# Moving the first weight columns to SyncE's queue, and reordering the start of an attention and feed-forward kernel

## The chip, the cores and the metric

One core of a Trainium2 chip. The metric is the device time of one execution in microseconds (us), lower is better. A profile gives the span of one execution; the timed value is about 2 us above the span. TensorE multiplies, VectorE and ScalarE copy and scale, GpSimd issues most DMAs, SyncE a few. In profile lines these are PE, DVE, ACT, POOL and SP; PEld is TensorE's weight load.

## The reference

Chunked attention (chunks of 32 tokens, 16 to the left and 8 to the right, 8 memory tokens), then a feed-forward part with a gate.

```python
for c in range(nc):                                   # batch 4, heads 8, 768 tokens, head size 64
    k_full = concatenate([mem_k, k[:, :, l_start:r_end]], axis=2)
    v_full = concatenate([mem_v, v[:, :, l_start:r_end]], axis=2)
    scores = matmul(q_c, k_full.T) / sqrt(64)
    out[:, :, c_start:c_end] = matmul(softmax(scores), v_full)
x = out.transpose(0, 2, 1, 3).reshape(3072, 512)
gate, val = maximum(x @ w_gate, 0), x @ w_val         # 512 x 1536 each
y = (gate * val) @ w_out                              # 1536 x 512
```

## The kernel before

Tokens go in 8 blocks of 384; heads go in pairs (`hp` 0 to 3). Everything in question is the first block, block 0, ahead of which nothing runs. Its rows of q, k and v (`rq`, `rk`, `rv`) come from GpSimd's queue, which casts f32 to f16 on the way; the first two heads come through SyncE and ScalarE as f32 (`kst`, `qst`), to start sooner. GpSimd's DMAs in order:

```python
load_k(0, 2, 2)                       # block 0, from head 2, 2 heads
load_rows_mem(pool_dma, ...)          # memory keys
load_q(0, 2, 2)
load_k(0, 4, 4)                       # the last four heads in one piece
load_q(0, 4, 4)
pool_dma(rv[0:KR], ...)               # the values of all 8 heads in one piece
load_rows_mem(pool_dma, rv[KR:KR + 2], 0, 0, H, mem_v)
load_w(0, 256)                        # the first 256 columns of wg and wv
load_w(256, 512)
# ... selection masks, the rows of block 1, further weights
```

`turn_pe` transposes rows of a head pair on TensorE, `step_s0` makes the scores and the exponentials, `wide_d` the sums (two ScalarE passes follow: log, then exponential), `gather_v` picks the value windows, `wide_v` multiplies by them, and VectorE scales the result into `xT`. The feed-forward part then takes `xT` in `chunk(0, f)`, four matmuls of the first two column blocks each; `fill` is a matmul whose result nobody reads.

```python
turn_pe(0, 1); turn_copy(0, 1)
step_s0(0, 0); step_s0(0, 1)
turn_pe(0, 2); turn_copy(0, 2)
wide_d(0, 0)
turn_pe(0, 3); turn_copy(0, 3)
step_s0(0, 2)
wide_d(0, 1)
step_s0(0, 3)
gather_v(0)                           # windows 0, 1 of all heads: 8 matmuls, one VectorE copy
wide_d(0, 2)
gather_v(2)                           # windows 2, 3
# ...
wide_v(0, 0)
wide_v(0, 1, xo2[:, 0, 0:TB])
# ... GpSimd's further loads
ffn_open(0, (0, 1))
wide_d(0, 3)
wide_v(0, 2)
chunk(0, 0); chunk(0, 1)
wide_v(0, 3, xo2[:, 1, 0:TB])
chunk(0, 2); chunk(0, 3)
```

The softmax here doesn't subtract the row's maximum and nothing guards it: scores larger than these inputs give would overflow.

Of the kernel before, what the change touches and what calls it, by code (L numbers as in the profile page):

```python
# [8 lines left out]
F32 = mybir.dt.float32  # L9
# [8 lines left out]
def kernel(  # L18
# [12 lines left out]
    nc = tc.nc  # L31

    B, H, S, D = q.shape
# [7 lines left out]
    TB = 384  # L41
    NB = B * S // TB
    NQ = 4
# [3 lines left out]
    J = 4  # L47
    QR = TB // J
    KR = 112
    NFC = DM // 128  # L50
# [3 lines left out]
    NEG = -30000.0  # L54

    const = ctx.enter_context(tc.tile_pool(name="const", bufs=1))
    half = ctx.enter_context(tc.tile_pool(name="half", bufs=2))
    turned = ctx.enter_context(tc.tile_pool(name="turned", bufs=2))
    epool = ctx.enter_context(tc.tile_pool(name="epool", bufs=4))
# [10 lines left out]
    sp = nc.sync.dma_start  # L70
    act_dma = nc.scalar.dma_start
    pool_dma = nc.gpsimd.dma_start
    dve_copy, act_copy = nc.vector.tensor_copy, nc.scalar.copy
# [2 lines left out]

    ident = const.tile([128, 128], F16, name="ident")
    sels = [const.tile([128, NQ, 32], F16, name=f"sel{p}") for p in range(2)]
    kst = const.tile([KR + 2, 2, J * D], F32, name="kst")
    qst = const.tile([QR, 2, J * D], F32, name="qst")  # L80
    k16s = [const.tile([128, NQ, H, D], F16, name=f"k16{p}") for p in range(2)]

    vwins = [const.tile([128, NQ, H, 2 * D], F16, name=f"vwin{p}") for p in range(2)]
# [3 lines left out]
    rv = const.tile([KR + 2, H, J * D], F16, name="rv")  # L87
# [39 lines left out]
    def load_k(n, h0, nh):  # L127
        pool_dma(rows_of(n)[0][0:KR, h0:h0 + nh], k_rows(n, h0, nh))  # L128

    def load_q(n, h0, nh):  # L130
        pool_dma(rows_of(n)[1][:, h0:h0 + nh], q_rows(n, h0, nh))

    def load_rows(n, h0, nh):
        load_k(n, h0, nh)
        load_q(n, h0, nh)
# [35 lines left out]
    def load_w(c0, c1):  # L171
        for dst, src in ((wg, moe_w_gate), (wv, moe_w_val)):
            pool_dma(dst[:, :, c0:c1], src.rearrange("(c p) f -> p c f", p=128)[:, :, c0:c1])
# [10 lines left out]
    def turn_pe(n, hp):  # L184
        if n != 1:
            pool, tag = (pools["t"], "t") if n == 0 else (pools["s"], "sc")
            ps = pool.tile([128, 2, 512], F32, tag=tag, name="kq_ps")
            kps, qps = ps[:, 0], xs if (n, hp) == (0, 0) else ps[:, 1, 0:TB]
        else:
            ps, kps, qps = None, bank("k_ps"), bank("q_ps")[:, 0:TB]  # L190
        turns[n, hp] = ps, kps, qps
        rk, rq = (t.rearrange("p h (j d) -> p h j d", j=J) for t in rows_of(n))
        sel = sels[n % 2].rearrange("p i t -> p (i t)")


        ksteps, qsteps = (dst.rearrange("p (j r) -> p j r", j=J) for dst in (kps, qps))
        if n == 0:
            ksteps = kps.rearrange("p (i j t) -> p j i t", i=NQ, j=J)
            qsteps = qps.rearrange("p (r j) -> p j r", j=J)
        for t, steps, w in ((rk, ksteps, sel[0:KR + 2]), (rq, qsteps, ident[:QR, :QR])):  # L200
            for j in range(J):
                for hh in range(2):
                    nc.tensor.matmul(steps[D * hh:D * hh + D, j], lhsT=t[:, 2 * hp + hh, j], rhs=w,  # L203
                                     start=True, stop=True)

    def turn_copy(n, hp):
        if n not in kTs:
            kq = turned.tile([128, HP, 512 + TB], F16, tag="kq", name="kq")
            kTs[n] = kq[:, :, 0:512].rearrange("p a (i m) -> p i a m", i=NQ)
            qTs[n] = kq[:, :, 512:].rearrange("p a (i m) -> p i a m", i=NQ)  # L210
            turns[n] = kq
        ps, kps, qps = turns.pop((n, hp))
        if n == 0 and hp == 0:
            dve_copy(turns[n][:, hp, 0:512], kps)
            act_copy(q00, qps)
        elif n == 0:
            dve_copy(turns[n][:, hp], ps.rearrange("p a c -> p (a c)")[:, 0:512 + TB])
        else:
            for src, dst in ((kps, turns[n][:, hp, 0:512]), (qps, turns[n][:, hp, 512:])):
                dve_copy(dst.rearrange("p (r j) -> p r j", j=J), src.rearrange("p (j r) -> p r j", j=J))  # L220
# [29 lines left out]
    def step_s0(n, hp):  # L250

        sc = pools["t"].tile([128, 2, 512], F32, tag="t", name="sc_ps")
        mq = bass.AP(tensor=maskq.tensor, offset=maskq.offset, ap=[maskq.ap[0], [0, NQ], [1, QB]])
        for hh in range(2):
            nc.tensor.matmul(sc[:, hh, 0:TB].rearrange("p (i m) -> p i m", m=QB), lhsT=maskk, rhs=mq,
                             start=True, stop=False)
        score_mms(n, hp, sc, False)
        ex = epool.tile([128, 2, NQ, QB], F16, tag="ex", name="ex")
        nc.scalar.activation(ex.rearrange("p h i m -> p h (i m)"), sc[:, :, 0:TB], ACT.Exp, scale=SCALE)
        exs[n, hp] = ex  # L260
# [25 lines left out]
    def wide_d(n, hp):  # L286
        ex = exs[n, hp]
        for i0, i1, kind in ((0, 1, 1), (1, NQ, 0)) if n == 0 else ((0, NQ - 1, 0), (NQ - 1, NQ, 2)):
            for hh in range(2):
                nc.tensor.matmul(xs[D * hh:D * hh + D, QB * i0:QB * i1], lhsT=ones[:, kind, :],  # L290
                                 rhs=ex[:, hh, i0:i1, :], start=True, stop=True)
        rinv = rpool.tile([128, TB], F32, tag="rw", bufs=4, name="rw")
        nc.scalar.activation(rinv, xs, ACT.Ln, scale=1.0 / 64.0)
        nc.scalar.activation(rinv, rinv, ACT.Exp, scale=-1.0, bias=mln64)
        rinvs[n, hp] = rinv

    def wide_v(n, hp, xo_=xo):
        ex = exs.pop((n, hp))
        for i in range(NQ):
            for hh in range(2):  # L300
                nc.tensor.matmul(xo_[D * hh:D * hh + D, QB * i:QB * i + QB], lhsT=vwins[n][:, i, 2 * hp + hh, 0:D],
                                 rhs=ex[:, hh, i, :], start=True, stop=True)
        nc.vector.tensor_tensor(out=x_of(n)[:, hp, :], in0=xo_, in1=rinvs.pop((n, hp)), op=ALU.mult)  # L303
# [87 lines left out]
    def fill(count):  # L391
        for i in range(count):
            nc.tensor.matmul(xo, lhsT=filler[:, 0:128], rhs=filler[:, 0:TB], start=True, stop=True)
# [36 lines left out]
    def build_sel(p):  # L430
# [4 lines left out]
        for i0, i1, t0, t1 in parts:  # L435
# [7 lines left out]
    load_k(0, 2, 2)  # L443
    load_rows_mem(pool_dma, rows_of(0)[0][KR:KR + 2, 2:H], 0, 2, H - 2)
    load_q(0, 2, 2)
    load_k(0, 4, 4)
    load_q(0, 4, 4)
    pool_dma(rv[0:KR], bass.AP(tensor=v.tensor, offset=v[0, 0, 0, 0].offset,
                               ap=[[J * D, KR], [S * D, H], [1, J * D]]))
    load_rows_mem(pool_dma, rv[KR:KR + 2], 0, 0, H, mem_v)  # L450
    load_w(0, 256)
    load_w(256, 512)

    def one_words(p, r0, r1, i0, i1, what):
# [6 lines left out]
    def chunk(n, f):  # L461
        for x in range(2):
            for a in range(2):
                ffn_mm(n, x, f, a)


    with tc.tile_pool(name="tps", bufs=3, space=bass.MemoryType.PSUM) as pools["t"]:
        def gather_v(i0):

            ps = pools["t"].tile([128, 2, 512], F32, tag="t", name="vg_ps")  # L470
            for i in range(2):
                for j in range(J):
                    nc.tensor.matmul(ps[32 * j:32 * j + 32, i].rearrange("p (h d) -> p h d", h=H),
                                     lhsT=sels[0][0:KR + 2, i0 + i, :], rhs=rv[:, :, D * j:D * j + D],
                                     start=True, stop=True)
            dve_copy(vwins[0][:, i0:i0 + 2, :, 0:D].rearrange("p i h d -> p (i h) d"),  # L476
                     ps.rearrange("p i (h d) -> p (i h) d", h=H))

        fill(11)

        for j in range(J):
            nc.tensor.matmul(xo[32 * j:32 * j + 32, 0:D], lhsT=sels[0][0:KR + 2, 0, :], rhs=ones[0:KR + 2, 0, :],
                             start=True, stop=True)
        dve_copy(rows_of(0)[0][0:KR + 2, 0:2], kst)
        act_copy(rows_of(0)[1][:, 0:2], qst)
        dve_copy(ones[:, 1], xo[:, 0:D])
        turn_pe(0, 0)
        turn_copy(0, 0)
        turn_pe(0, 1)
        turn_copy(0, 1)  # L490
        step_s0(0, 0)
        step_s0(0, 1)
        turn_pe(0, 2)
        turn_copy(0, 2)
        wide_d(0, 0)
        turn_pe(0, 3)
        turn_copy(0, 3)
        step_s0(0, 2)
        wide_d(0, 1)
        step_s0(0, 3)  # L500
        gather_v(0)
        wide_d(0, 2)
        gather_v(2)
    pools["f"] = ctx.enter_context(tc.tile_pool(name="fps", bufs=4, space=bass.MemoryType.PSUM))
    pools["s"] = ctx.enter_context(tc.tile_pool(name="sps", bufs=1, space=bass.MemoryType.PSUM))
    xo2 = pools["s"].tile([128, 2, 512], F32, tag="sc", name="xo2_ps")
# [1 line left out]
    wide_v(0, 1, xo2[:, 0, 0:TB])  # L508
    zero(vwins[1][96:128, NQ - 1, :, 0:D], 0.0)


    build_sel(1)
    load_rows_mem(pool_dma, rows_of(1)[0][KR:KR + 2], 1, 0, H)
# [10 lines left out]
    load_w(1024, 1280)  # L524

    ffn_open(0, (0, 1))
    wide_d(0, 3)
    wide_v(0, 2)
    chunk(0, 0)
    chunk(0, 1)  # L530
    wide_v(0, 3, xo2[:, 1, 0:TB])
    chunk(0, 2)
    chunk(0, 3)
    ffn_close(0)
# [128 lines left out]
```

## Time and profile before

| Kernel before | value |
|---|---|
| time, median of 4 runs | 240.34 us (239.27 to 240.90) |
| span of the profiled run | 238.6 us |
| granted clock, mean of the span | 0.992 |
| TensorE busy | 227.2 us, 95% |
| the 16 first feed-forward matmuls end, third column block begins | 22.07 us |

The prediction below shows the main lines: a start of 24 us with gaps, then a TensorE that never waits. Two more lines are of TensorE's timeline (start, length, instruction, count, and in brackets the idle time before it with what ended it), where the last four heads' rows arrive:

```profile
9.11 0.41 PE L203 MATMUL kq_ps<-sel,rk 114*64 114x128 f16 x8 [0.71 <-DMA rk<-in_k_dram]
10.10 0.52 PE L203 MATMUL kq_ps<-ident,rq 96*64 96x96 f16 x8 [0.57 <-DMA rq<-in_q_dram]
```

Keys at 9.1, queries at 10.1 us, with waits of 0.7 and 0.6 us.

### The profile page before, as it was taken

The numbers are of one execution on the slowest core, as the hardware profiler recorded it, in microseconds if no ns is written. First come the engines' busy times: TensorE is split into PE (matmuls) and PEld (weight loads), VectorE is DVE, ScalarE is ACT, GpSimd is POOL, SyncE is SP. The second block draws the span as 40 slices with busy tenths as digits, with TensorE's granted clock in tenths as the row PEclk, the third lists the DMA queues.
The fourth block names the chain that finished last, engine by engine and source line by source line (L and its number), as shares of the span: only waits on it lengthen the run. The fifth ranks groups of instructions, "written<-read, shape, count | busy, mean of one in ns | idle before, by whom it ended". The sixth has DMA issues, their size and how long they took to land.

```text
span 238.6 us, 4626 instructions
## 1 busy us (share of the span) xinstructions
PE 227.2 (95%) x1751; PEld 131.7 (55%) x1751; DVE 107.8 (45%) x209; ACT 141.4 (59%) x299; POOL 101.5 (43%) x131
## 2 busy tenths in 40 slices
PE   7769788999999999999999999999999999999993
PEld 4435545665644566546664566556664666455641
DVE  3465915789721055612662146505551266313400
ACT  3563495357762388827984499628892798434320
POOL 8959967946039800991099105960220000000000
PEclk9988999999999999999999999999999999999999
DMA  6999999999999999499939992999802100120012
GB/s 114 144 194 195 196 170 178 166 191 153 152 131 137 195 139 140 31 166 171 164 21 156 128 178 45 94 175 142 115 0 85 50 0 0 47 88 0 1 47 88
DMA packets 104220, 27.35 MB, mean 115 GB/s; under 512 B 87206, under 2 KB 101254, under 8 KB 104198
## 3 DMA queue, kind: packets, MB, share of 16 engines
q0 software_dynamic: 79904, 15.36, 79.2%
q1 hardware_dynamic: 20630, 5.33, 19.4%
q10 hardware_dynamic: 3664, 6.36, 8.0%
q8 instruction: 14, 0.23, 0.4%
q14 instruction: 8, 0.07, 0.1%
HBM read 31.13 MB, written 6.29 MB: 157 GB/s over the span
## 4 chain that ended last, share of the span: by engine, by line
PE 85%; DMA 4%; ACT 3%; DVE 3%; POOL 2%; issue 1%; POOLq 0%; DVEq 0%; ACTq 0%
PE g_ps L346 26%; PE v_ps L346 25%; PE o_ps L372 25%; DMA rv<-in_mem_v_dram 3%; PE sc_ps L272 3%; PE xo_ps L310 2%; ACT ex L278 2%; PE xs_ps L310 2%; DVE vwin L476 1%; PE kq_ps L203 1%; DMA out_dram<-o_sb 1%; PE sc_ps L247 1%; DVE gv L353 1%; POOL rk L128 1%; DVE xT L303 1%
## 5 line engine op out<-in xcount | busy, mean ns | idle before, releaser
L353 DVE TENSOR_TENSOR gv<-v_ps,gr 128x384 f16<-128x384 f32 x95 | 52.8, 557 | 97.3 <-ACT gr L352 84.3
L346 PE MATMUL g_ps<-xT,wg 128*128 128x384 f16 x380 | 78.9, 328 | 1.0 <-DVE kq L220 1.0
L346 PE MATMUL v_ps<-xT,wv 128*128 128x384 f16 x380 | 78.7, 327 | 0.0
L372 PE MATMUL o_ps<-wo,gv 128*128 128x512 f16 x288 | 63.5, 379 | 0.0
L352 ACT ACTIVATE gr<-g_ps 128x384 f16<-128x384 f32 x95 | 46.1, 487 | 24.5 <-PE g_ps L346 13.4
L346 PEld LDWEIGHTS <-wg 128*128 128x128 f16 x384 | 36.8, 98 | 24.0 <-issue 1.5
L346 PEld LDWEIGHTS <-wv 128*128 128x128 f16 x384 | 36.3, 98 | 22.0 <-issue 0.5
L372 PEld LDWEIGHTS <-gv 128*128 128x128 f16 x288 | 28.0, 98 | 32.9
L234 POOL COPY qbd<-qT 64x1536 f16<-64x1536 f16 x10 | 14.6, 1464 | 59.1 <-DMA qT<-q16n 58.8
L381 ACT COPY o_sb<-o_ps 128x512 f32<-128x512 f32 x23 | 13.5, 587 | 39.0 <-PE o_ps L372 33.0
L278 ACT ACTIVATE ex<-sc_ps,bias 128x256 f16<-128x256 f32 x84 | 33.3, 468 | 2.1 <-PE sc_ps L247 1.4
L143 POOL DMA_DIRECT2D vwin<-in_v_dram x28 | 25.2, 905 | 2.0 <-PE v_ps L346 1.2
L319 ACT ACTIVATE rinv<-ln,mln 64x768 f32<-64x768 f32 x24 | 22.2, 926 | 0.0
L314 ACT ACTIVATE ln<-xo_ps 64x384 f32<-64x384 f32 x24 | 11.7, 488 | 16.2 <-PE xs_ps L310 16.2
L143 POOL DMA_DIRECT2D k<-in_k_dram x20 | 17.9, 904 | 0.0
L325 DVE TENSOR_TENSOR xT<-xo_ps,rinv 64x384 f16<-64x384 f32 x24 | 13.1, 547 | 10.1 <-ACT rinv L319 10.0
L169 POOL DMA_DIRECT2D q16n<-in_q_dram x20 | 15.5, 779 | 4.9 <-DMA wo<-in_moe_w_out_dram 4.9
L325 DVE TENSOR_TENSOR xT<-xs_ps,rinv 64x384 f16<-64x384 f32 x24 | 13.2, 551 | 0.7
L310 PEld LDWEIGHTS <-vwin 128*128 128x128 f16 x192 | 10.6, 98 | 3.0
L314 ACT ACTIVATE ln<-xs_ps 64x384 f32<-64x384 f32 x24 | 11.4, 477 | 0.0
L310 PE MATMUL xo_ps<-ex,vwin 128*128 128x96 f16 x96 | 11.1, 206 | 0.0
L310 PE MATMUL xs_ps<-ex,vwin 128*128 128x96 f16 x96 | 11.1, 206 | 0.0
(85 smaller groups left out, 138.0 us busy)
## 6 DMA issues: line engine op xcount, KB each, us to landing
out_dram<-o_sb ACTq DMA_DIRECT2D x23, 256.0 KB
vwin<-in_v_dram POOLq DMA_DIRECT2D x21, 120.0 KB, 8.5
q16n<-in_q_dram POOLq DMA_DIRECT2D x20, 96.0 KB, 5.0
k<-in_k_dram POOLq DMA_DIRECT2D x15, 120.0 KB, 4.2
wg<-in_moe_w_gate_dram POOLq DMA_DIRECT2D x6, 256.0 KB, 8.0
wv<-in_moe_w_val_dram POOLq DMA_DIRECT2D x6, 256.0 KB, 8.5
wo<-in_moe_w_out_dram POOLq DMA_DIRECT2D x3, 512.0 KB, 9.2
rk<-in_k_dram POOLq DMA_DIRECT2D x5, 224.0 KB, 6.7
```

Of the source, the lines that this page charges most:

```text
L143: pool_dma(dsts[p][NMEM + m0:NMEM + m1, i, :, 0:D], src)
L169: pool_dma(q16s[n][:, i], src)
L234: nc.gpsimd.tensor_copy(qbds[n % 2][s, :, :, hh, :].rearrange("p i a m -> p (i a) m"), qTs[n][s].rearrange("p i a m -> p (i a) m"))
L278: nc.scalar.activation(flat[:, :, :, s], view[:, :, :, s], ACT.Exp, scale=SCALE, bias=bias[:, g:g + 1])
L310: nc.tensor.matmul((xo, xs)[hh][:, QB * i:QB * i + QB], lhsT=vw[:, i, 2 * hp + hh, :], rhs=ex[:, hh, i, :], start=True, stop=True)
L314: nc.scalar.activation(ln[:, hh], (xo, xs)[hh][D:128], ACT.Ln, scale=1.0 / 64.0)
L319: nc.scalar.activation(rinv, lns.pop((n, hp)), ACT.Exp, scale=-1.0, bias=mln64[0:D, :])
L325: nc.vector.tensor_tensor(out=x_of(n)[D * hh:D * hh + D, hp, :], in0=(xo, xs)[hh][0:D], in1=rinv[:, hh, :], op=ALU.mult)
L346: nc.tensor.matmul(ps[a], lhsT=(wg, wv)[a][:, f, 128 * m:128 * m + 128], rhs=xTs[n][:, f, :], start=(f == 0), stop=(f == NFC - 1))
L352: nc.scalar.activation(gr, g_ps, ACT.Relu)
L353: nc.vector.tensor_tensor(out=gvs[n][:, m, :], in0=v_ps, in1=gr, op=ALU.mult)
L372: nc.tensor.matmul(o_ps, lhsT=gvs[n][:, m, 128 * t:128 * t + 128], rhs=wo[:, m, :], start=(m == 0), stop=(m == NDC - 1))
```

## The change

The intent: get the first weights out of GpSimd's queue, where they stand behind the values, by bringing them as f32 through SyncE into the buffers of the first rows, with a cast on GpSimd; let the first half of the heads go on when half of the values is there; and take the sums out of the way of the first feed-forward matmuls.

```diff
-    kst = const.tile(...); qst = const.tile(...)
+    kst, qst = (stage.tile([128, 1024], F32, tag="st", name=nm)...)      # pool of 2 buffers
...
-    load_k(0, 4, 4)
-    load_q(0, 4, 4)
-    pool_dma(rv[0:KR], ...)                        # 8 heads
+    load_rows(0, 4, 2)
+    load_rows(0, 6, 2)
     load_rows_mem(pool_dma, rv[KR:KR + 2], 0, 0, H, mem_v)
-    load_w(0, 256)
+    for h0 in (0, 4):
+        pool_dma(rv[0:KR, h0:h0 + 4], ...)         # 4 heads each
     load_w(256, 512)
...
+        def stage_w(dst, src):
+            st = stage.tile([128, 1024], F32, tag="st", name="w32")...
+            sp(st, src...[:, :, 0:256])
+            first_w.append((dst, st))
+        def gather_v(h0):                           # 16 matmuls: 4 windows of 4 heads
...
         turn_copy(0, 1)
+        stage_w(wg, moe_w_gate)
+        stage_w(wv, moe_w_val)
         step_s0(0, 0)
         step_s0(0, 1)
+        wide_d(0, 0)
         turn_pe(0, 2)
         turn_copy(0, 2)
-        wide_d(0, 0)
+        wide_d(0, 1)
         turn_pe(0, 3)
         turn_copy(0, 3)
         step_s0(0, 2)
-        wide_d(0, 1)
+        fill(2)
         step_s0(0, 3)
         gather_v(0)
         wide_d(0, 2)
-        gather_v(2)
+        gather_v(4)
+        fill(3)
+        wide_d(0, 3)
...
+    for dst, st in first_w:
+        nc.gpsimd.tensor_copy(dst[:, :, 0:256], st)
...
     ffn_open(0, (0, 1))
-    wide_d(0, 3)
     wide_v(0, 2)
+    wide_v(0, 3, xo2[:, 1, 0:TB])
     chunk(0, 0)
     chunk(0, 1)
-    wide_v(0, 3, xo2[:, 1, 0:TB])
     chunk(0, 2)
     chunk(0, 3)
```

More of the change, by code (lines that the diff above doesn't have):

```diff
@@ L56 @@
     const = ctx.enter_context(tc.tile_pool(name="const", bufs=1))
+    stage = ctx.enter_context(tc.tile_pool(name="stage", bufs=2))
     half = ctx.enter_context(tc.tile_pool(name="half", bufs=2))
@@ L78 @@
     sels = [const.tile([128, NQ, 32], F16, name=f"sel{p}") for p in range(2)]
-    kst = const.tile([KR + 2, 2, J * D], F32, name="kst")
-    qst = const.tile([QR, 2, J * D], F32, name="qst")
+    kst, qst = (stage.tile([128, 1024], F32, tag="st", name=nm)[0:rows, 0:2 * J * D].rearrange("p (h c) -> p h c", h=2)
+                for nm, rows in (("kst", KR + 2), ("qst", QR)))
     k16s = [const.tile([128, NQ, H, D], F16, name=f"k16{p}") for p in range(2)]
@@ L445 @@
     load_q(0, 2, 2)
-    load_k(0, 4, 4)
-    load_q(0, 4, 4)
-    pool_dma(rv[0:KR], bass.AP(tensor=v.tensor, offset=v[0, 0, 0, 0].offset,
-                               ap=[[J * D, KR], [S * D, H], [1, J * D]]))
+    load_rows(0, 4, 2)
+    load_rows(0, 6, 2)
     load_rows_mem(pool_dma, rv[KR:KR + 2], 0, 0, H, mem_v)
-    load_w(0, 256)
+    for h0 in (0, 4):
+        pool_dma(rv[0:KR, h0:h0 + 4], bass.AP(tensor=v.tensor, offset=v[0, h0, 0, 0].offset,
+                                              ap=[[J * D, KR], [S * D, 4], [1, J * D]]))
     load_w(256, 512)
@@ L467 @@
     with tc.tile_pool(name="tps", bufs=3, space=bass.MemoryType.PSUM) as pools["t"]:
-        def gather_v(i0):
-            ps = pools["t"].tile([128, 2, 512], F32, tag="t", name="vg_ps")
-            for i in range(2):
+        first_w = []
+        def stage_w(dst, src):
+            st = stage.tile([128, 1024], F32, tag="st", name="w32").rearrange("p (c f) -> p c f", c=NFC)
+            sp(st, src.rearrange("(c p) f -> p c f", p=128)[:, :, 0:256])
+            first_w.append((dst, st))
+        def gather_v(h0):
+            ps = pools["t"].tile([128, 2, 512], F32, tag="t", name="vg_ps").rearrange("p a (i c) -> p (a i) c", i=2)
+            for i in range(NQ):
                 for j in range(J):
-                    nc.tensor.matmul(ps[32 * j:32 * j + 32, i].rearrange("p (h d) -> p h d", h=H),
-                                     lhsT=sels[0][0:KR + 2, i0 + i, :], rhs=rv[:, :, D * j:D * j + D],
+                    nc.tensor.matmul(ps[32 * j:32 * j + 32, i].rearrange("p (h d) -> p h d", d=D),
+                                     lhsT=sels[0][0:KR + 2, i, :], rhs=rv[:, h0:h0 + 4, D * j:D * j + D],
                                      start=True, stop=True)
-            dve_copy(vwins[0][:, i0:i0 + 2, :, 0:D].rearrange("p i h d -> p (i h) d"),
-                     ps.rearrange("p i (h d) -> p (i h) d", h=H))
+            dve_copy(vwins[0][:, :, h0:h0 + 4, 0:D], ps.rearrange("p i (h d) -> p i h d", d=D))
         fill(11)
```

## The prediction

> **What bounds the kernel now.** I read the page's first lines, then the busy time by stretches, the chain of waits of the first 24 us, TensorE's timeline there, and the DMA view of single stretches. By stretches (columns: TensorE, weight loads, VectorE, ScalarE, GpSimd, granted clock, DMA share, GB/s):
>
> ```profile
> 13.00:16.40 3.40, 1.87 (x32) 0.55 (x25) 2.22 (x2) 2.70 (x6) 2.13 (x4) 1.00 1.45 197
> 16.40:19.80 3.40, 3.12 (x30) 1.89 (x31) 1.99 (x5) 1.11 (x2) 2.68 (x6) 0.50 1.46 193
> ...
> 24.00:45.00 21.00, 17.80 (x208) 10.81 (x203) 12.75 (x27) 12.63 (x30) 16.63 (x22) 1.00 1.74 176
> 45.00:236.00 191.00, 189.82 (x1326) 110.24 (x1324) 82.68 (x150) 117.73 (x252) 64.99 (x70) 1.00 0.99 102
> ```
>
> The reader sees two kernels in one. From 45 us on TensorE works 189.82 of 191.00 us, and the list of its waits there is empty: nothing that this change touches can shorten that part. Before it TensorE has gaps, and between 16.4 and 19.8 us it runs at half clock. A microsecond saved before the first feed-forward matmul is saved at the end only if nothing between 24 and 45 us takes it back. The chain of waits says what sets that start:
>
> ```profile
> 5.29 0.78 POOL rv L448
> 6.08 7.31 DMA rv<-in_mem_v_dram
> 13.39 0.14 issue
> 13.52 0.64 PE vg_ps L473 x8
> 14.16 0.02 issue
> 14.18 2.37 DVE vwin L476 x2
> ...
> 16.59 0.39 PE xo_ps L301 x4
> ...
> 17.08 0.57 DVE xT L303
> ...
> 18.22 0.43 PE g_ps L346
> 18.66 0.32 PE v_ps L346
> ...
> 20.09 0.16 PE g_ps L346
> ```
>
> Values land at 13.39 us; gathers, two copies of 1.2 us one after the other, and the first x tile fill the time until 18.2. The matmuls' step is 0.32 us at half clock, 0.16 at full. TensorE's timeline puts the end of the 16 matmuls of the first two column blocks at 22.07. So 13.39 to 22.07, 8.7 us, is the stretch that the change rewrites. The DMA view says how busy the transfers are, in 4 to 12 us, then in 16 to 25 us:
>
> ```profile
> DMA packets 2369, 1.09 MB, mean 136 GB/s; under 512 B 247, under 2 KB 2369, under 8 KB 2369
> ```
>
> ```profile
> DMA packets 3665, 1.75 MB, mean 195 GB/s; under 512 B 244, under 2 KB 3665, under 8 KB 3665
> ```
>
> Only the software queue (GpSimd's) works in both. The page's DMA row stays at 9 from about 6 to 95 us: every byte of the weights waits behind another.
>
> **What the skill says.** "DMA: Bandwidth & Descriptors", section "Queues, rings and completion order": each DMA engine takes turns between its queues, packet by packet; section "SWDGE vs HWDGE vs iDMA": only GpSimd's DMAs can cast. So moving the weights to SyncE's queue needs f32 in SBUF and a cast, and it does not make a new path: it lets 1 MB overtake in the same 16 engines. The trace of before has too little of two queues at once to show the turns. "TensorE: Matmul & The Clock Gate", Part 1: the clock is halved after a window of some 3.4 us without enough work, and the page speaks of an idle window. Here TensorE was busy 1.87 of 3.40 us and was halved all the same, for the next 3.4 us; the measurement decides, half-busy is not enough. "SBUF — State Buffer", section "Who interferes with whom": a VectorE instruction with at most one SBUF input and outside the two-port modes does not block GpSimd. VectorE's copies at issue read PSUM, so I expect the new casts not to hold them up; the trace before has no pair large enough to show it.
>
> **The change, part by part.**
>
> 1. Weights. Two software loads go (GpSimd 0.83 + 0.81 us of issue, 256 KB each as written). In their place SyncE issues two loads of 512 KB f32 once the first rows' stage is read: VectorE's cast ends at 4.87 us, ScalarE's at 5.15. The first rows' own packets came about 1.1 us after their issue at 0.81, so the weights flow from about 6.2 us. They are 1024 packets of 1 KB.
>
> 2. Casts. GpSimd's cast of 8x512 f32 to f16 took 604 ns, 1.2 ns an element, its copy of 64x1536 f16 1464 ns, 0.95. For 128x1024 I take 1.2 us, two make 2.4 us. They lie after the weight issues, at about 10.6 us in GpSimd's order, and everything after them (next block's rows, the next weights) waits until they are done.
>
> 3. GpSimd's issues. The rest of the rows come in four pieces for two, the values in two for one: three more issues of about 0.75 us, and two gone. The values' last issue ends near 9.0 us for 6.7.
>
> 4. When the values land. Ahead of the end of the values lie 344 + 288 + 456 KB, 1.11 MB. Before, 1.09 MB had moved between 4 and 12 us, and the release came at 13.39: about 1.4 us from the last byte to the release (estimate). Now by 6.2 us some 0.25 MB (about 500 packets of 512 B) have moved. I take 390 packets a microsecond for both queues together (16 to 25 us: 3665 in 9 us is 407 with the small ones), half for each: the weights take 1024/195 = 5.2 us, to 11.4. The software queue is then at about 1520 of its 2172 packets; the last 652, alone at 350, need 1.9 us, to 13.3; landing 14.6. The first half of the values (packet 1724) lands at about 13.3, the last query rows (1260) at 11.4, the second weight at 12.8. So the values come 1.2 us LATER than the 13.39 of now. This is the price.
>
> 5. What follows the landing. Query rows at 11.4; turning 0.75, copy 1.09 (128x896), scores 0.4: gather of the first head half 13.5 to 14.2, its copy 14.2 to 15.4; the second gather waits for 14.6, its copy is 15.4 to 16.6. Then x tiles of 0.55 us: first at 17.2, second 17.75. The sums of all head pairs are ahead of this, so the third and fourth value matmuls (0.3 us each) follow the first x tile: 17.2 to 17.8. The 16 matmuls start at 17.8 without a break, and end 16 times 0.163 later, at 20.4, if the clock is full. Before: 22.07. Gain 1.65 us. The three kinds of things in it: no half clock under the first 11 matmuls (11 x 0.16 = 1.8 us in the best case, of which wide gaps would have hidden some), the sums and last values taken out of their middle (about 0.9 us: 17.08 to 17.65 and 20.34 to 20.64), minus 1.2 us of later values.
>
> 6. Fillers. Five matmuls, 0.16 us each at full clock, 0.8 us, in time in which TensorE waits for data. I count them zero, but for the clock.
>
> 7. Casts against later loads. Casts: first from 11, second 12.8 to 14.0. Then the selection for the other kind of block 0.7, and the next block's rows 0.66 + 0.76 + 0.68: two of the four row loads are issued by 16.8 for 14.2 now, the rest by 18.2. All software bytes ahead of them are through at about 16, so the queue runs dry for up to 1 us; then 416 KB at 195 GB/s take 2.2 us: landed at about 20.5. They are needed 1.4 us after 20.4, at 21.8. The next weights (needed 29.1 now, 27.4 then; issued from 19) have 4 us to spare. I take off 0.25 us for what some of this costs.
>
> Sum: 1.65 - 0.25 = 1.4 us, of 240.35: **239.0 us**.
>
> **The rivals.**
>
> (a) Turns are uneven: SyncE's packets get more than half, or the common rate is lower. Then rows and values slip further, the values to 15.8 us, the gain falls to about 0.4 (240.0), or to a small loss. For it: 136 GB/s for the rows before 12 us against 195 later, so the start is not at full rate even alone. Against: this low rate with one queue may be just the room that a second queue fills.
>
> (b) That room: the rows keep their pace, the values land near 13.4, gathers and copies end near 15.6, the matmuls end at 19.3, gain 2.8 us. Then the next block's rows (20.5) are the new wait, 20.6 being when they are needed: 237.6 to 238.
>
> (c) GpSimd becomes the bound: if the second weight lands at 15 or later, the casts end at 17.4, the next rows arrive at 22.5 or later and TensorE waits there; result 240 to 241. The lead of 1.5 us in step 7 speaks against it.
>
> (d) It is all hidden: VectorE's copies hold TensorE for 1.0 us at 25.4 and ScalarE for 0.74 at 35.6, and if these ends stayed fixed in time, the gain would vanish. But both chains hang on the same first matmuls and move with them.
>
> **Range and chances.** (a) and (c) bound it above at some 240.4, (b) below at 237.4. Before's own runs span 239.27 to 240.9, so the middle of the range is hardly wider than that. A gain of 2% is 4.8 us, more than half of the whole 8.7 us stretch, and no rival gives it; a loss of 4.8 us needs the values later by 7 us. Faster 0.02, within 2% 0.97, slower 0.01.
>
> **What would show it.** In the changed profile: SyncE's loads at about 5 us, their queue's bytes ending near 11.4 (step 4); the values landing 1 us or more after 13.4; casts of 1.2 us each (2); granted clock 1.00 or a shorter halved stretch (5); the end of the 16 first matmuls at 20.4; no TensorE wait for next block's rows at 21 to 23 us (7); and 45 us onwards as full as now, only earlier. If the values land before 13.4, step 4 is wrong; if the casts take over 2 us or VectorE's copies grow, step 2; if the first matmuls gain 1.6 us and the end does not, something between 24 and 45 us took it.

## The result, and the profile after

The changed kernel takes 242.95 us in the median of 4 runs (242.08 to 243.45) against 240.34, where 239.0 was predicted, and the range ended at 240.4. The ratio is 1.011, 95% interval 1.0064 to 1.0156. (Ratios here are the mean time of one kernel's runs over that of the other's runs of the same rounds, so not quite the ratio of the medians quoted. Executions over 1.5% slower than the fastest of the same kernel are left out of the means.) The change costs about 1%: it is slower, by less than 2%.

The profiled run is the fastest of the four: 240.3 us of span for 238.6, 1.7 us more. The other three have spans of 240.7, 241.1 and 241.3 us, with mean granted clocks of 0.985, 0.986 and 0.983 for 0.990.

TensorE's timeline of the changed kernel, at the place of the two lines of before:

```profile
11.90 0.41 PE L204 MATMUL kq_ps<-sel,rk 114*64 114x128 f16 x8 [1.48 <-DMA rk<-in_k_dram]
13.17 0.52 PE L204 MATMUL kq_ps<-ident,rq 96*64 96x96 f16 x8 [0.85 <-DMA rq<-in_q_dram]
```

The keys of the last heads come 2.8 us later than before, their queries 3.1 us later. The chain of waits of the changed kernel (start, length, what) says what hangs on them:

```profile
5.76 7.36 DMA rq<-in_q_dram
...
13.17 0.52 PE kq_ps L204 x8
13.69 0.66 PE sc_ps L256 x2
14.34 0.44 PE sc_ps L248 x8
14.78 0.75 PE xo_ps L394 x2
15.53 0.64 PE sc_ps L256 x2
16.17 0.43 PE sc_ps L248 x8
16.60 0.84 PE vg_ps L482 x11
17.44 0.29 PE xs_ps L291 x4
17.73 0.55 PE vg_ps L482 x16
18.28 0.59 PE xo_ps L394 x3
...
20.98 0.36 PE xo_ps L302 x8
21.34 0.27 PE g_ps L347
```

Before, the first item was the landing of the values at 13.39 us. Now it is the landing of the last query rows at 13.12, and behind it stand the turning and the scores of the last heads, which used to be done by then, and after them fillers (the lines of `xo_ps L394`), gathers and sums. The values come late as well: by the trace's semaphore records their halves land at 16.44 and 17.31 us, the first one 0.1 us before the gathers begin at 16.53. The feed-forward matmuls start at 21.27 us on TensorE's timeline for 18.16, run at 0.16 us each without a break, and end at 23.88 for 22.07: 1.8 us later. The span is 1.7 us longer. So in these two profiles all of the loss is made in the first 24 us, and nothing after gives or takes.

By stretches (columns as in the prediction: TensorE, weight loads, VectorE, ScalarE, GpSimd, granted clock, DMA share, GB/s):

```profile
9.60:13.00 3.40, 1.23 (x20) 0.73 (x20) 1.09 (x1) 2.02 (x5) 0.33 (x1) 1.00 1.12 230
13.00:16.40 3.40, 3.23 (x30) 1.43 (x30) 1.09 (x1) 0.81 (x1) 1.92 (x2) 0.61 1.42 206
16.40:19.80 3.40, 2.93 (x57) 1.56 (x52) 2.30 (x3) 2.48 (x5) 3.40 (x9) 0.89 0.86 109
...
45.00:236.00 191.00, 191.00 (x1335) 111.21 (x1334) 83.28 (x151) 117.56 (x253) 69.60 (x75) 1.00 1.02 105
```

TensorE worked only 1.23 us of the 3.40 in which it waited for rows, and was given a clock of 0.61 in the next stretch: the halved stretch has not gone, it has moved. By the clock records of the traces it lies from 13.76 to 17.17 us, where it lay from 16.37 to 19.78: 2.6 us earlier, from under the feed-forward matmuls to under the scores and the gathers.

The DMA view of 7 to 12 us shows both queues at once; q1 is SyncE's, q0 GpSimd's (packets, MB, share of 16 engines):

```profile
DMA packets 1311, 1.03 MB, mean 206 GB/s; under 512 B 64, under 2 KB 1311, under 8 KB 1311
...
q1 hardware_dynamic: 776, 0.78, 57.8%
q0 software_dynamic: 535, 0.25, 39.0%
```

262 packets a microsecond, 59% of them SyncE's. In the version below that leaves SyncE's weights out (soft_w), GpSimd's queue alone, in the same 5 us, shows:

```profile
q0 software_dynamic: 1456, 0.65, 110.7%
```

So the two queues together move more bytes (1.03 MB for 0.65), SyncE's packets being larger, but fewer packets, and GpSimd's queue, with the rows and the values in it, moves 921 packets less. And the casts, on GpSimd's timeline:

```profile
13.41 1.04 POOL L525 CAST wg<-w 128x1024 f16<-128x1024 f32 x1 [3.48 <-DMA w<-in_moe_w_gate_dram]
15.52 1.04 POOL L525 CAST wv<-w 128x1024 f16<-128x1024 f32 x1 [1.07 <-DMA w<-in_moe_w_val_dram]
```

They take 1.04 us each, but GpSimd stands still for 3.48 and 1.07 us until there is something to cast. The last weights are ready at 16.6 us, 4.7 us before they can be used: they had no need to overtake anything. (In soft_w, where they stand behind the values again, TensorE takes them at 17.57 us without a wait.)

### The profile page after: what moved, and what is told of

It reads as the page before. It is cut to its first block, busy times and chain, and to the rows that moved or that the text cites. A ratio compares the mean times of both kernels' runs of the same rounds, so it can differ in the third digit from the quotient of the medians.

```text
span 240.3 us, 4674 instructions
## 1 busy us (share of the span) xinstructions
PE 228.6 (95%) x1772; PEld 133.0 (55%) x1772; DVE 107.6 (45%) x209; ACT 141.1 (59%) x299; POOL 103.9 (43%) x134
## 4 chain that ended last, share of the span: by engine, by line
PE 86%; DMA 4%; ACT 4%; DVE 2%; POOL 2%; issue 1%; POOLq 0%; DVEq 0%; ACTq 0%
PE g_ps L347 25%; PE o_ps L373 25%; PE v_ps L347 25%; DMA rq<-in_q_dram 3%; PE sc_ps L273 3%; PE xo_ps L311 2%; ACT ex L279 2%; PE xs_ps L311 2%; PE sc_ps L248 1%; PE kq_ps L204 1%; POOL rk L129 1%; DMA out_dram<-o_sb 1%; DVE gv L354 1%; ACT rw L294 1%; DVE xT L304 1%
## 5 line engine op out<-in xcount | busy, mean ns | idle before, releaser
L235 POOL COPY qbd<-qT 64x1536 f16<-64x1536 f16 x10 | 14.6, 1462 | 57.6 <-DMA qT<-q16n 57.3
L315 ACT ACTIVATE ln<-xo_ps 64x384 f32<-64x384 f32 x24 | 11.7, 487 | 16.4 <-PE xs_ps L311 16.4
L326 DVE TENSOR_TENSOR xT<-xo_ps,rinv 64x384 f16<-64x384 f32 x24 | 13.1, 547 | 10.1 <-ACT rinv L320 10.0
L315 ACT ACTIVATE ln<-xs_ps 64x384 f32<-64x384 f32 x24 | 11.4, 475 | 0.0
```

The costliest lines, as they stand in the source:

```text
L235: nc.gpsimd.tensor_copy(qbds[n % 2][s, :, :, hh, :].rearrange("p i a m -> p (i a) m"), qTs[n][s].rearrange("p i a m -> p (i a) m"))
L315: nc.scalar.activation(ln[:, hh], (xo, xs)[hh][D:128], ACT.Ln, scale=1.0 / 64.0)
L326: nc.vector.tensor_tensor(out=x_of(n)[D * hh:D * hh + D, hp, :], in0=(xo, xs)[hh][0:D], in1=rinv[:, hh, :], op=ALU.mult)
```

## The experiments

All ran in rounds beside the kernel before. Every output was correct. Each variant has 6 runs; one of soft_nofill (242.19 us) is in its median and not in its ratio. In the rounds of the variants the kernel before had 11 runs each and medians of 240.84 (soft_w, only_hw, no_fill, hw_late), 240.66 (half_hw, fill_wait, soft_nofill, casts_only) and 240.36 us (the last four), so medians of different rows compare only roughly; ratios compare within a round. In the table, "third block" is the time at which TensorE begins the third column block in the profiled run, that is, when the 16 first matmuls are over.

| Kernel | median us | ratio (95%) | third block | span | difference |
|---|---|---|---|---|---|
| before | 240.34 | 1 | 22.07 | 238.6 | 216.5 |
| changed | 242.95 | 1.011 (1.006 to 1.016) | 23.88 | 240.3 | 216.4 |
| soft_w | 238.57 | 0.991 (0.987 to 0.995) | 20.18 | 236.7 | 216.5 |
| only_hw | 244.08 | 1.012 (1.007 to 1.017) | 26.00 | 242.4 | 216.4 |
| no_fill | 243.56 | 1.014 (1.008 to 1.019) | 24.95 | 241.3 | 216.4 |
| hw_late | 244.98 | 1.019 (1.014 to 1.025) | 24.51 | 241.4 | 216.9 |
| half_hw | 242.65 | 1.008 (1.003 to 1.012) | 23.82 | 240.3 | 216.5 |
| fill_wait | 242.41 | 1.008 (1.003 to 1.012) | 24.47 | 240.8 | 216.3 |
| soft_nofill | 238.81 | 0.992 (0.987 to 0.996) | 20.63 | 237.2 | 216.6 |
| casts_only | 238.26 | 0.989 (0.986 to 0.993) | 20.00 | 236.5 | 216.5 |
| hw_mid | 242.68 | 1.009 (1.005 to 1.013) | 24.61 | 241.0 | 216.4 |
| soft_oldrows | 239.32 | 0.996 (0.993 to 0.998) | 20.37 | 236.9 | 216.5 |
| sums_only | 239.92 | 0.999 (0.996 to 1.002) | 22.18 | 238.7 | 216.5 |
| halves_only | 240.51 | 1.001 (0.997 to 1.005) | 20.67 | 237.2 | 216.5 |

The last column is span minus third block. It is 216.3 to 216.6 us in all but one kernel: whatever these variants do, they do before the third column block. The exception, hw_late, is explained below. A profile is one run, and the start varies from run to run, so ratios decide and profiles explain.

What varies can be read from the mean granted clock that every run lists. One stretch of 3.41 us at half clock, as in the trace of before, takes 0.007 from the mean of a 239 us run. The 33 runs of the kernel before in these rounds fall into three groups: 15 with a mean clock of 0.999 or 1.000 took 239.27 to 240.36 us (median 239.79), 13 with 0.992 or 0.993 took 240.54 to 241.42 (240.85), five with 0.986 took 241.66 to 242.40 (242.14). So a halved stretch goes with 1.1 to 1.3 us, and the median of before depends on how many of its runs had one; why some have and some have not is not shown. Of soft_w's six runs (0.998 to 1.000) none had one: it gains about 1.2 us on the full-clock runs of before, and the rest of its 2.3 us is clock that before often loses.

**soft_w: the weights back on GpSimd's queue, the rest of the change kept.** The main theory (A): SyncE's weights overtake the last rows. The rival (B): the new order on TensorE, with its fillers, costs the time.

```diff
-        stage_w(wg, moe_w_gate)
-        stage_w(wv, moe_w_val)
-    load_w(256, 512)
+    load_w(0, 256)
+    load_w(256, 512)
```

> The changed kernel with its first 256 weight columns back on GpSimd's casting queue, behind the values, and no casts on GpSimd; row pieces, gathers by head halves, sums ahead and fillers stay. Theory A (SyncE's weights overtake the last rows): the last query rows land near 10.5 us again (13.1 in the changed kernel), the 16 first matmuls end at 19.5 to 21 us (23.9 changed, 22.1 before), the time is 1 to 2.5 us under before, ratio 0.990 to 0.996. Rival B (the new order on TensorE with its fillers costs the time): it stays at 1.005 to 1.012.

Ratio 0.991: the rest of the change is good, and this version beats both kernels. Its TensorE timeline at the same places, and where the values come:

```profile
9.85 0.42 PE L204 MATMUL kq_ps<-sel,rk 114*64 114x128 f16 x8
10.07 0.53 PE L204 MATMUL kq_ps<-ident,rq 96*64 96x96 f16 x8
...
13.10 0.62 PE L483 MATMUL vg_ps<-rv,sel 114*32 114x256 f16 x16 [0.77 <-DMA rv<-in_v_dram]
```

No wait for rows is left (no brackets), the values set the start again, and a half of them is enough at 13.1 us. B falls: the same order with the same fillers gains.

**only_hw: only the weights' new path, on the kernel before.**

```diff
-    load_w(0, 256)
+        stage_w(wg, moe_w_gate)        # after turn_copy(0, 1)
+        stage_w(wv, moe_w_val)
+    for dst, st in first_w: nc.gpsimd.tensor_copy(dst[:, :, 0:256], st)
```

> The kernel before with only the weights' new path (SyncE's f32 loads and GpSimd's casts), nothing else changed. Theory A: the last rows land at 13 us or later, the first feed-forward matmul comes 2 to 4 us later than before's 18.2, ratio 1.008 to 1.016, worse than the changed kernel's 1.011 or equal. Rival B: within 0.4% of before.

1.012, as A expected: this part alone makes the whole loss. The parts do not add up: 1.012 and soft_w's 0.991 would make 1.003, and the changed kernel has 1.011, so with the late rows the gain of the rest is gone. TensorE waits 2.4 us for the query rows, the first feed-forward matmul starts at 21.61 us (3.5 us late) and at half clock.

**no_fill: the changed kernel without its fillers.**

```diff
-        fill(2)
-        fill(3)
```

> The changed kernel without its two and three fillers. If the fillers lie on the path (0.75 and 0.59 us in its chain at half clock), up to 1.3 us come back: ratio 1.005 to 1.008, the 16 matmuls end near 22.6. If they keep the clock up as meant, their loss costs more half clock under the first matmuls and the ratio is 1.011 to 1.016.

1.014, not told apart from the changed kernel's 1.011. The fillers stand in the chain with 0.75 and 0.59 us, but without them nothing comes back; in its profile the clock is 0.53 in 13.0 to 16.4 us and 0.50 in 16.4 to 19.8. That profile's query rows also came 0.85 us later than the changed kernel's (turned at 14.01 for 13.17), so it can't say how much the fillers help; that they are the loss is ruled out.

**hw_late: the same two loads, later, from ScalarE's queue.** If overtaking is the trouble, issuing behind the rows should cure it.

```diff
-            sp(st, src...)
+            act_dma(st, src...)
-        stage_w(...) twice after turn_copy(0, 1)
+        stage_w(...) twice after wide_d(0, 1)
```

> The changed kernel with the same two f32 loads issued from ScalarE's queue after the second pair's sums (about 11 us) in place of SyncE at 5 us; casts and everything else stay. Theory A: last query rows land near 10.5 us, the halved stretch shrinks or goes, the values are delayed by what overtakes them then; the casts end at 17 to 19 us and set the first matmul; 16 matmuls end at 20.5 to 22, ratio 0.992 to 1.000. Rival C (the casts on GpSimd hold up the next loads): as slow as the changed kernel or slower, with TensorE waiting for the next block's rows near 22 to 25 us.

1.019, the worst of all (with an interval of 1.014 to 1.025 the record calls its class unclear), where A had expected 1.000 or less. The last rows and the values come on time: TensorE waits for neither. But the loads are issued at 11.62 and 12.14 us and move nothing for over 3 us. The DMA view of 12 to 15 us has packets of GpSimd's queue only (q8 is instruction fetch), that of 15.5 to 18.5 us has mostly ScalarE's, q10 (the first of them starts at 15.17):

```profile
q0 software_dynamic: 845, 0.42, 110.1%
q8 instruction: 1, 0.02, 2.0%
```

```profile
q10 hardware_dynamic: 989, 0.99, 92.9%
```

So the weights themselves are late: the first feed-forward matmuls wait for the casts, and most of the 16 run at half clock.

```profile
19.32 0.34 PE L347 MATMUL g_ps<-xT,wg 128*128 128x384 f16 x1 [0.80 <-POOL wg L525]
20.64 0.50 PE L347 MATMUL v_ps<-xT,wv 128*128 128x384 f16 x1 [0.98 <-POOL wv L525]
```

That puts the third block at 24.51 us, 2.4 us later than before. The third theory (C), that the casts on GpSimd hold up the next loads, is seen as well. Until the weights come GpSimd waits at its first cast and can't issue the next loads, so the DMA engines run dry:

```profile
18.22 1.04 POOL L525 CAST wg<-w 128x1024 f16<-128x1024 f32 x1 [8.29 <-DMA w<-in_moe_w_gate_dram]
```

```profile
19.80:24.00 4.20, 3.37 (x12) 1.68 (x13) 0.00 (x0) 0.00 (x0) 4.20 (x9) 0.59 0.19 13
```

13 GB/s in 19.8 to 24.0 us, where the kernel before moved 196. TensorE then waits 0.54 us twice for the next block's query rows, and 0.33 and 0.21 us for later weights: this is the one kernel whose last column in the table is longer, by 0.4 us. So of the 2.8 us that this profile is longer, C has 0.4 by this column. The profile is of the fastest of the six runs; two others with almost the same mean clock (0.992 for 0.993) took some 2 us more, and what they lose is open.

**half_hw: only the gate half on SyncE's queue.**

```diff
-        stage_w(wv, moe_w_val)
+    pool_dma(wv[:, :, 0:256], ...)     # GpSimd's queue, before load_w(256, 512)
```

> The changed kernel with only the gate half of the first columns on SyncE's f32 queue and cast by GpSimd; the value half goes back to GpSimd's casting queue behind the attention values. Theory A (bytes that overtake the rows set the loss): half the overtaking bytes, so the last query rows land between 10.2 us (weights on GpSimd's queue) and 13.1 (both on SyncE's), near 11.5, and the time lies about half way between 0.991 and 1.011: 0.997 to 1.005. If a second queue of any size breaks the pace of the first: 1.008 or more.

1.008, outside A's 0.997 to 1.005: half of the bytes, and most of the loss; the rows landed at 13.1 us again, where 11.5 was expected. The trace's semaphore records show how. These DMAs signal 16 times, and have landed with the last. For the last query rows the 16 came between 8.56 and 9.59 us in soft_w, between 11.85 and 13.12 in the changed kernel, and here 15 came between 10.21 and 11.89, half way, as A would have it; the sixteenth came at 13.10. That TensorE goes on with the last signal is shown; why it is so late is not. By the expectation's own ranges 1.008 is also what "a second queue of any size" would give. So whether the loss goes with the bytes that overtake or with a second queue as such is open; weights ahead of the rows in GpSimd's own queue, which would tell the two apart, were not tried.

**fill_wait: fillers where TensorE waits for rows.**

```diff
         wide_d(0, 1)
+        fill(8)
         turn_pe(0, 3)
```

> The changed kernel with eight more fillers just where TensorE waits for the last rows (before the fourth pair is turned), all else the same. If half clock is part of the loss: the granted clock stays 1.00 from 13 to 16.4 us (0.61 in the changed kernel), the chain after the last rows shrinks from 8.15 us by about 1 us, ratio 1.005 to 1.008. If the lateness of the rows is all of it: unchanged, 1.010 to 1.012.

1.008 against 1.011, intervals that overlap widely. The clock did what was expected, 1.00 in 13.0 to 16.4 us:

```profile
13.00:16.40 3.40, 2.41 (x36) 1.13 (x30) 1.09 (x1) 1.01 (x2) 1.04 (x1) 1.00 1.41 209
```

But a full clock brought TensorE to the gathers only to wait there for the values, 1.17 and 0.30 us. (The query rows landed at 13.9 us in this profile.) 1.008 is at the edge of what was expected if the halved clock is part of the loss. The clocks of the runs say more: four of the six had 0.999 or 1.000 and took 241.54 to 242.89 us, median 241.8, against 239.8 for the four runs of before in this round with such a clock. About 2 us of loss stand without any halved clock, so it is the smaller part, and rows and values are late together.

**soft_nofill and casts_only: two parts of soft_w that might matter.** The first takes the five fillers out of soft_w. The second puts two casts of 128x1024 f32 of other data at the place of the changed kernel's, without any wait for a landing.

```diff
 # soft_nofill
-        fill(2)
-        fill(3)
```

```diff
 # casts_only
+    for i in (0, 2):
+        nc.gpsimd.tensor_copy(wo[:, i:i + 2, :]..., zsrc)    # wo is overwritten by its load later
```

> The version with the weights on GpSimd's queue, without the two and three fillers. There TensorE waits for the values (0.8 and 0.25 us) and the fillers lie in waits. If they hold the clock: without them the clock falls to half in 16.4 to 19.8 us as in the kernel before, the 16 first matmuls end about 1 us later (21.2 for 20.2), ratio 0.994 to 0.997. If not needed: 0.990 to 0.992.

> The version with the weights on GpSimd's queue, with two GpSimd casts of 128x1024 f32 to f16 of other data at the place of the changed kernel's casts: the cost of the casts themselves, without their wait for a landing and without SyncE's traffic. Each 1.04 us; GpSimd's next loads are issued 2.1 us later; VectorE's copies of 1.2 us do not grow. If loads have slack (theory A): within 0.3% of 0.991. Rival C (casts hold up the next loads): 0.996 or more, with TensorE waiting for the next block's rows.

soft_nofill: 0.992, as soft_w's 0.991, so the fillers were not needed there for the gain; in the profile the clock stayed at 1.00 with TensorE busy 2.16 us of the stretch from 13.0 to 16.4. But two of its six runs lost clock (0.993, and 0.982 in the slow one), and none of soft_w's did, so whether the fillers make the full clock surer is open. casts_only: 0.989. The casts delay the next rows' issue by 2 us (first key rows at 14.54 us for 12.57 in soft_w) and the end does not move:

```profile
11.36 2.12 POOL L526 CAST wo<-wo 128x1024 f16<-128x1024 f32 x2
```

So C holds only for the wait ahead of a cast, not for the cast.

**hw_mid: the two loads issued at 6.4 and 6.9 us, between the rows' issues and the values'.** After hw_late a sharper form of A: packets of the second queue flow when the software packets that were issued before them are through, and then hold up what was issued after them.

```diff
-            sp(st, src...)
+            act_dma(st, src...)
-        stage_w(...) twice after turn_copy(0, 1)
+        stage_w(...) twice after turn_copy(0, 0)
```

> The changed kernel with the two f32 loads issued from ScalarE's queue after its first query copy, at about 6.9 us: after the last rows' issues on GpSimd's queue (end 6.4) and beside the values' (7.0 to 8.4), where SyncE issued at 5.1. Theory A2 (packets of the second queue flow once the software packets issued before them are through, and then hold up what was issued later): the last query rows land near 10.3 us as without SyncE's weights, and the values pay: they land at 16.5 to 18 us (about 13 without); 16 first matmuls end at 22.5 to 24, ratio 1.004 to 1.014. If the second queue slows all alike from its first packet: the rows are late too, 12 us or more.

1.009, and the damage moves as this says:

```profile
10.61 0.53 PE L204 MATMUL kq_ps<-ident,rq 96*64 96x96 f16 x8
...
16.75 0.62 PE L482 MATMUL vg_ps<-rv,sel 114*32 114x256 f16 x16 [3.87 <-DMA rv<-in_v_dram]
```

The rows are on time without a wait, though the last of them land at 10.43 us for 9.59 in soft_w, so what was issued before is not wholly spared. The values, 13.1 us in soft_w, come at 16.7, and TensorE waits 3.87 us for them. What the weights overtake depends on when they are issued; both times it was something that was needed sooner.

**soft_oldrows, sums_only, halves_only: which part of soft_w gains?** The first is soft_w with rows and values in the large pieces of before. The other two are the kernel before with one part each: the sums and the last value matmuls in the changed order; the gathers by head halves.

```diff
 # soft_oldrows
-    load_rows(0, 4, 2); load_rows(0, 6, 2); values in two pieces
+    load_k(0, 4, 4); load_q(0, 4, 4); values in one piece
```

```diff
 # sums_only: wide_d(0, 0), wide_d(0, 1) ahead of the turns, wide_d(0, 3) after gather_v(2), wide_v(0, 3) ahead of chunk(0, 0)
 # halves_only: gather_v(h0) as in the change, called with 0 and 4
```

> The version with the weights on GpSimd's queue (0.991), with the rows and values in the larger pieces of the kernel before. If the smaller pieces matter: half of the values can't come first, first gather at 13.5 in place of 13.1 and copies 0.4 us later, ratio 0.992 to 0.995. If three GpSimd issues less pay as much: 0.990 to 0.992.

> The kernel before with only the sums ahead of the values (and the third and fourth value matmuls ahead of the first blocks' chunks). The sums and last values leave the middle of the 16 matmuls, but the second gather's copies still hold the first value matmul and the clock is still halved from 16.4: saves 0.3 to 1 us, ratio 0.996 to 0.999.

> The kernel before with only the gathers by head halves. Both copies still run before the first x tile on VectorE, so only the value matmuls of the first half move under the second copy: saves 0.2 to 0.6 us, ratio 0.997 to 1.000.

0.996, 0.999 and 1.001. Neither part alone can be told from before. Both together, with the fillers, give 0.996, and the smaller pieces seem to add the rest, though the intervals of 0.996 and 0.991 just overlap. Part of the 0.996 is clock: all six runs of soft_oldrows have 0.998 or more. At 1.000 sums_only's four runs (239.49 to 239.97 us) are no faster than before's six of that round (239.27 to 240.36). halves_only holds a warning. Its profile looks as good as soft_w's, with a third block at 20.67 us and full clock:

```profile
16.40:19.80 3.40, 3.02 (x40) 1.88 (x41) 2.56 (x6) 1.11 (x2) 1.82 (x6) 1.00 1.46 193
```

Yet this run took 239.33 us, the fastest of its six, whose median is 240.51. Its profile shows what a run is worth whose clock is not halved, and nothing of the kernel's usual run. The mean clocks of the other five, 0.997 to 0.986, tell that most lost clock (the slowest, 241.92 us, has the lowest), but not where.

## Why the prediction was wrong, point by point

- **What bounds the kernel: right.** It said that nothing after 45 us can be shortened and asked whether 24 to 45 us would take a gain back. The last column of the table answers: what happens in the first 24 us reaches the end unaltered.
- **Step 4, the landings: this is the step that failed.** It said "I take 390 packets a microsecond for both queues together (...), half for each", and from it "the last query rows (1260) at 11.4", the second weight at 12.8. Measured in 7 to 12 us: 262 a microsecond, 59% of them SyncE's, so 107 a microsecond for the software queue where 195 were counted. The query rows landed at 13.1 us, the second weight at 15.5, the halves of the values at 16.4 and 17.3 for 13.3 and 14.6. The 390 were taken from 16 to 25 us, although the view of 4 to 12 us, on the same page of the prediction, showed 2369 packets in 8 us, 296 a microsecond. The sign of the effect was seen (the values "1.2 us LATER", "This is the price"), its size was not: the values came 2.7 to 3.1 us later still, and the last query rows paid too.
- **Step 5, what follows the landing.** The 16 matmuls at full clock without a break, 2.6 us: right. The way from the query rows to the first matmul was put at 6.4 us (11.4 to 17.8) and took 8.15 (13.12 to 21.27). The missing 1.75 us are work at half clock between 13.8 and 17.2, and fillers. But they hid behind the values, which landed only 0.1 us before the gathers began. Counted from the first half of the values, step 5 was nearly right: from 16.44 to 23.88 are 7.4 us, for 7.1 predicted (13.3 to 20.4) and 7.1 in soft_w (13.06 to 20.18). So nearly all of the 3.5 us by which the end was missed is step 4. "If the clock is full" was made true for the wrong stretch: by waiting for rows TensorE lost it earlier. fill_wait shows that this part alone, mended, buys little: the values are the next wait. One sum of step 5 is wrong by its own chain: before, five of the first matmuls ran at half clock (18.22 to 19.93) and not 11, worth 0.8 us and not up to 1.8; and its three terms make 1.5, not 1.65.
- **Step 6, fillers at zero.** In the chain of the changed kernel they stand with 1.34 us. no_fill shows that taking them away brings nothing back, so zero was right in effect, though not for the reason given (that TensorE waits for data there; it did not).
- **Step 2, the casts: right.** 1.04 us each for the estimated 1.2. VectorE's copy of 128x896, 1.09 us, was 1.09 beside the first cast, too. casts_only confirms that they cost nothing.
- **Step 7 and rival (c).** No wait for the next block's rows: right, if only because TensorE itself was late. The danger named in (c), GpSimd waiting for the weights, is real: in hw_late it costs some 0.4 us, on top of the first matmuls' own wait for the casts.
- **Rival (a), uneven turns and a lower common rate, was the right one,** and was given "about 0.4 (240.0), or (...) a small loss". Its own evidence, 136 GB/s before 12 us, should have led: with the measured 107 a microsecond in step 4's working the query rows come at 14.6 (6.2 + 760/107 + 1.3), past the 13.1 measured, and not at 11.4. What was small in it was the loss, 2.6 us in the medians. **Rival (b),** that the low rate leaves room for a second queue, is refuted by 921 packets fewer in 5 us.

## What to carry to other kernels

Here a second DMA queue was no second path: before moving a load to it, list what is in flight at the moment of issue and what will be issued next, and ask which of these is needed first; here 1 MB that was needed at 21 us overtook rows that were needed at 10. Take the rate of a transfer from the stretch in which it will run, not from the best stretch of the trace. Compare runs of the same mean clock before you give a difference a cause. And when a change has several parts, undo the one that touches the shared resource first: without it, the rest of this change gains 0.9%, and with it the whole loses 1.1%.

## What the Trainium skill lacked or had wrong

- "DMA: Bandwidth & Descriptors", section "Latency and other measured facts", gives about 600 ns to the first byte of a load on SyncE's or ScalarE's queue. Here ScalarE's loads issued at 11.6 us moved no packet between 12 and 15 us, while GpSimd's queue worked off what it had been given before. The page does not say for how busy an engine its time holds; a wait behind another queue's earlier packets is not on it.
- The same page, section "Queues, rings and completion order", says that each engine takes turns between queues packet by packet, and counts several descriptors to a packet; it gives no shares and no start. Equal turns in the profile's packets from the moment of issue, as the prediction had them, do not fit: hw_late had 3 us without one packet of the second queue, and in the changed kernel the shares were 59% and 41% of the packets, 0.78 and 0.25 MB, in 7 to 12 us. Whether the profile's packets are the page's is not shown. Turns that begin after the earlier packets fit hw_late and, but for the rows' 0.8 us, hw_mid; the mechanism itself is not shown.
- The same page, section "Why a DMA increments its semaphore by 16 and not by 1", has the 16 signals of a DMA but no figure for how far apart they come: 1.0 us in soft_w for the last query rows, 1.3 us in the changed kernel, 2.9 us in half_hw.
- "TensorE: Matmul & The Clock Gate", Part 1, speaks of an idle window before the clock is halved. Here the clock was halved after stretches that were far from idle. In every trace the clock's changes lie whole multiples of 3.41 us apart; in the stretches of that length just ahead of a halved one TensorE was busy 1.91 us (before), 1.86 (sums_only), 1.08 (changed), and in only_hw even 2.10 and 2.02, while 1.97 (fill_wait) and 2.08 (soft_nofill) were not followed by one. So a limit, if busy time sets it, lies near 2 us of the 3.41, and the profile's busy times do not place it closer.
